# Retention attention and a gated feed-forward layer in one kernel: another layout for the fourth block, another order in the queues

## The chip, the cores and the metric

The kernel runs on one core of a Trainium2 chip. The metric is the time of one execution on the device in microseconds (us); a comparison takes the median of several runs. A profile of one execution gives the times of the single instructions. TensorE (PE) multiplies matrices, VectorE (DVE), ScalarE (ACT) and GpSimd (POOL) work on elements, SyncE (SP) issues most of the DMA transfers.

## The reference

q, k and v have 8 batches, 8 heads, 576 positions and 64 columns in float32. Scores are q times k transposed over the root of 64, each multiplied by gamma(head) to the power of the distance and cut to the causal half; they multiply v. The result, as 4608 tokens of 512 columns, goes through a layer of 2048 hidden columns with h * cos(h):

```python
ret = scores * Dmat[None, :, :, :]          # gamma ** (i - j) for i >= j, else 0
x = np.matmul(ret, v).transpose(0, 2, 1, 3).reshape(4608, 512)
h = x @ w_in
out = (h * np.cos(h)) @ w_out
```

## The kernel before

The 4608 tokens are cut into 18 blocks j of 256 tokens (two chunks of 128), and into nine tiles n of 512 tokens (blocks 2n and 2n + 1) for the feed-forward layer. Blocks are counted from 0 here, so the fourth block is block 3.

For each block: load (L135 and L149) brings q, k and v in float32 through SyncE's queue; prep (scaled, L167) multiplies q and k by powers of gamma on GpSimd into bf16 tile qks; round_v (L178) makes v bf16; a transpose makes qkT from qks, either as one DMA of SyncE (transpose_dma, L197) or as eight TensorE transposes for each of q and k with a copy out of PSUM (transpose_pe, L210 and L215). scores (L244 or L282) multiplies keys with queries into PSUM, and VectorE multiplies by the mask into ret (L255 and L262, or L292). sums_of (L319) multiplies keys with values; VectorE adds the result to a running sum (L338, or L349 for each chunk), which ScalarE rounds into sb (L359). out_own (L375) multiplies ret with v, out_carried (L407) multiplies queries with the rounded sum, both into one PSUM bank, which outputs copies into xT on ScalarE (L430).

Blocks below NP_B hold two neighbouring tokens of k and v in a partition ("pair"): one DMA with pieces of 512 bytes, and 64 rows in each matmul of sums and own parts. The others hold one key and value a partition: a DMA for each chunk with pieces of 256 bytes, and 128 rows in a matmul. q always has two tokens a partition.

For each tile n: mm1 (L445) multiplies x with w_in, ScalarE makes cos (L457), VectorE multiplies both into gT (L460). The second product (mm2_seven, product, L563) works on a two by two split of gT and w_out with seven products in the order given by xs; w_sums and g_sum (L503) make the sums of quarters that it needs. g_sum runs on VectorE, but one of the four sums of each tile runs on GpSimd in pieces of two: number 3 for n = 1 and number 7 for n above 1. The tile n = 0 takes a plain second product instead (L927), with todo naming what else is issued after how many of its matmuls, and ends in copies of four row groups to tiles ot (L937).

Results leave through tiles ot of a pool of two buffers for each tag:

```python
op = ctx.enter_context(tc.tile_pool(name="op", bufs=2))
```

For n = 0 the four row groups take tags "a", "b", "c", "d" in turn. For n = 1, where products run in the order 2, 4, 6, 5, 7, 3 after an earlier 1, copied (L593, ScalarE) takes c11 from tag "a", p2 from "d", c21 from "c", u1 from "b" and c22 from "d"; adds (L589) follow on VectorE, and store issues two DMAs of SyncE for each (L579).

The schedule is written by hand: every engine runs its instructions in the order in which the program issues them, and waits only on semaphores. step(j) issues prep, the DMA transpose and round_v of the next block and then the load of a later one; sums_after(n, i) issues pieces of sums after the i-th group of mm1; at[...] puts scores, sums and outputs of the next blocks ahead of single products. A DMA on SyncE uses one of eight semaphores in turn, and waits for the DMA eight before it.

Of the kernel before, what the change touches and what calls it, by code (L numbers as in the profile page):

```python
# [13 lines left out]
ALU = mybir.AluOpType  # L14
# [3 lines left out]
def kernel(  # L18
# [9 lines left out]
    nc = tc.nc  # L28
    P = 128
# [17 lines left out]
    last = NT - 1  # L47
    BK = 256
    NB = NTOK // BK
    NP_B = 4  # L50
    PERQ = 9
    PERK = 9
    MIX = PERK // 2
# [133 lines left out]
    def prep(j):  # L187
        for name in "kq" if j < NP_B else "qk":
            for y in range(2):
                scaled(nc.gpsimd, j, name, y)  # L190
# [12 lines left out]
    def transpose_pe(j, name, bank, evac, ys=(0, 1)):  # L203
        if ("qkT", j) not in tiles:
            new_qkT(j)
        m = "qk".index(name)
        ps = psum.tile([P, len(ys), HG, P], BF16, tag=bank, name="tr")
        for u, y in enumerate(ys):
            for hg in range(HG):
                nc.tensor.transpose(  # L210
                    ps[:, u, hg, :],
                    tiles["qks", j][:, m, y, hg].rearrange("s a d -> s (a d)"),
                    ident,
                )
        evac(tiles["qkT", j][:, m, ys[0] : ys[-1] + 1], ps)  # L215
# [13 lines left out]
    def scores(j, banks):  # L229
        cs = chunks[j]  # L230
        kT = tiles["qkT", j]
        ret = retp.tile([P, 2, HG, 2, P], BF16, tag="ret", name="ret")
        pss = [
            psum.tile([P, HG, 2, P], F32, tag=t, name="sc")
            if isinstance(t, str)
            else [psum.tile([P, HG, P], F32, tag=u, name="sc") for u in t]
            for t in banks
        ]
        if cs[0].pair:
            order = [(c, y, he, hg) for hg in range(HG) for y in range(2) for he in range(2) for c in cs]  # L240
            mask = mask_mix if any(c.mixed for c in cs) else mask_p
            for c, y, he, hg in order:
                ps = pss[he]
                nc.tensor.matmul(  # L244
                    ps[y][c.rows, hg, :] if isinstance(ps, list) else ps[c.rows, hg, y, :],
                    lhsT=kT[he * D : he * D + D, 1, y, hg, c.rows],
                    rhs=q_cols(c, he, hg),
                    start=True,
                    stop=True,
                )  # L250

            def masked(he):
                if isinstance(pss[he], list):
                    for y in range(2):
                        nc.vector.tensor_tensor(  # L255
                            out=ret[:, he, :, y, :],
                            in0=pss[he][y],
                            in1=mask[:, y].unsqueeze(1).to_broadcast([P, HG, P]),
                            op=ALU.mult,
                        )  # L260
                    return
                nc.vector.tensor_tensor(  # L262
                    out=ret[:, he].rearrange("p b r i -> p b (r i)"),
                    in0=pss[he].rearrange("p b r i -> p b (r i)"),
                    in1=mask.rearrange("p r i -> p (r i)").unsqueeze(1).to_broadcast(
                        [P, HG, 2 * P]
                    ),
                    op=ALU.mult,
                )
        else:  # L270
            ret = ret.rearrange("p a b r i -> p (a b r i)").rearrange(
                "p (k a b i) -> p k a b i", k=2, a=2, b=HG
            )
            pss = [
                ps.rearrange("p b r i -> p (b r i)").rearrange("p (a b i) -> p a b i", a=2, b=HG)
                for ps in pss
            ]
            for c in cs:
                for hg in range(HG):
                    for i0 in range(0, P, HP):  # L280
                        for he in range(2):
                            nc.tensor.matmul(  # L282
                                pss[c.k][i0 : i0 + HP, he, hg, :],
                                lhsT=kT[he * D : he * D + D, 1, c.k, hg, i0 : i0 + HP],
                                rhs=q_cols(c, he, hg),
                                start=True,
                                stop=True,
                            )

            def masked(k):  # L290
                mask = mask_cmix if cs[k].mixed else mask_c
                nc.vector.tensor_tensor(  # L292
                    out=ret[:, k].rearrange("p a b i -> p (a b) i"),
                    in0=pss[k].rearrange("p a b i -> p (a b) i"),
                    in1=mask.unsqueeze(1).to_broadcast([P, H, P]),
                    op=ALU.mult,
                )

        tiles["ret", j] = ret
        return [lambda: masked(0), lambda: masked(1)]  # L300
# [213 lines left out]
    def sums_after(n, i):  # L514
        if n == 1:
            slots = {5: ((5, 0, 4),), 6: ((6, 0, 4),)}
        else:
            slots = {
                2: ((7, 0, 4),),
                3: ((5, 0, 4),),  # L520
                4: ((6, 0, 4), (7, 4, 6)),
                5: ((3, 0, 4),),
                6: ((5, 4, 6), (7, 6, E2)),
            }
        for x in slots.get(i, ()):
            g_sum(n, *x)
# [46 lines left out]
    def stored_rows(r0, c0, c1, t, queues=(nc.sync, nc.sync)):  # L573

        rows = out[r0 : r0 + P * t.shape[1], c0:c1].rearrange(
            "(j i r) c -> r i j c", r=2, i=HP
        )
        for r in range(2):
            queues[r].dma_start(rows[r], t[r * HP : (r + 1) * HP])  # L579
# [85 lines left out]
    def load_next(**kw):  # L665
        nonlocal loaded
        if loaded < NB:
            load(loaded, **kw)
            loaded += 1

    def step(then_load=True):

        nonlocal prepared
        if prepared < NB:
            prep(prepared)
            transpose_dma(prepared)
            round_v(prepared)
            prepared += 1
            if then_load:
                load_next()  # L680

    def steps_to(j):
        while prepared < min(NB, j):
            step()
# [128 lines left out]
    w_dma.append(load_w_out(12))  # L813
    scaled(nc.gpsimd, 2, "q", 0)
    load_next(names="kqv", gate=w_dma[6])
    load_next()
    prepared = 4

    def intro(j, sc_banks, st_bank, put_off=None, then=None):
        add = sums_of(j, st_bank)  # L820
# [44 lines left out]
    for n in range(NT):  # L865
        blocks = blocks_of.get(n) or [(e + k * E2, 0, W) for e in range(0, E2, 2) for k in range(2)]
        for i, (et, c0, cw) in enumerate(blocks):
            inside = {
                (0, 1): {2: block1_carried},
                (1, 0): {2: lambda: transpose_pe(3, "q", "b", act)},  # L870
                (1, 2): {3: block3_scores},
                (1, 3): {2: lambda: sums_of(3, "st")()()},
            }.get((n, i), {})
            off = [] if (n, i) == (1, 3) else None
            between = block1_sums if (n, i) == (0, 0) else None
            mm1(n, et, c0, cw, banks_of.get(n, "abmabmab")[i], inside, off, between)
            if (n, i) == (0, 0):
                block1_own()
            if (n, i) == (1, 0):
                step(False)  # L880
                load_next()
                for r0, ot in stores:
                    stored_rows(r0, 0, DM, ot)
            if (n, i) == (1, 1):
                step(False)
                load_next()
                step()
            if (n, i) == (1, 3):
                mm2_seven(1, {}, None, (1,), lambda: (outputs(3, "m"), off.pop()()))
            if n:  # L890
                sums_after(n, i)
            if (n, i) == (2, 6):
                step()
        if n == 0:
            gT = tiles["g", n]
            two = psum.tile([P, 2, DM], F32, tag="m", name="o")
# [6 lines left out]
                (37, lambda: round_v(2)),  # L903
                (42, block2_scores),
                (50, block2_sums),
                (50, lambda: prep(3)),
                (57, load_next),
                (59, lambda: round_v(3, (act, act))),
                (60, lambda: outputs(2, "b")),
                (62, lambda: transpose_pe(3, "k", "a", act)),  # L910
            ]
            todo += [
                (at, lambda x=x, e=e: w_sums(x, e, e + 4))
# [51 lines left out]
        def first_scores(flush, pend):  # L965
            g_sum(n, 5, 4, E2)
            g_sum(n, 6, 4, E2)
            masks = scores(a, "ab")
            add_a = sums_of(a, "st")
            add_b = sums_of(b, "m")  # L970
            masks[0]()
            add_a()()
            masks[1]()
            g_sum(n, 3, 0, E2)
            g_sum(n, 7, 0, 4)
            tiles["rounded"] = add_b()
            g_sum(n, 7, 4, E2)

        def next_scores(flush, pend):
            outputs(a, "a")  # L980
# [30 lines left out]

        def stored(u):
            if n == 1:
                steps_to({2: 8}.get(u, 0))
            else:
                steps_to({0: 2 * n + 6, 3: 2 * n + 7}.get(u, 0))

# [31 lines left out]
```

## Time and profile before

| | |
|---|---|
| median of three runs | 296.8 us (295.59 to 297.94) |
| profiled execution | 296.28 us, span 294.6 us |
| granted TensorE clock, mean | 0.994 |
| busy: PE, DVE, ACT, POOL | 283.2, 215.6, 143.0, 145.6 us |
| DMA queue of SyncE | 44.84 MB, 75.6% of 16 engines over the span |
| DMA transposes | 14, median 5.1 us from issue to landing |

The span is the time from the first to the last instruction of the profile; the rest of the execution's time lies around it. Busy times count work only, not waiting or the issue of DMAs. A timeline row gives start, duration, engine, line, operation, output<-inputs, shape and count, and in brackets the idle time of the engine before it with what ended it. Lines are those of the kernel before.

### The profile page before, as it was taken

The page shows a single profiled execution, that of the slowest core. Times are in us where ns is not written, and L with a number is a line of the kernel's source. Part 1 is how long each engine was busy: PE and PEld are TensorE (multiplying, and loading weights), DVE is VectorE, ACT ScalarE, POOL GpSimd, SP SyncE. Part 2 cuts the span into 40 slices and gives each one's busy share as a digit, 9 for nine tenths or more (in the row PEclk, how much of TensorE's full clock was granted, in tenths as well). Part 3 has the DMA queues.
Part 4 walks back from the last instruction along what each step waited for, and adds up shares of the span by engine and source line. Part 5 has one row for each costly group of instructions (what it writes and reads, how often), then busy time and mean ns, then how long its engine had stood idle before and what let it go on. Part 6 is the DMA issues. An engine that isn't in the chain of part 4 may idle for free.

```text
span 294.6 us, 7623 instructions
## 1 busy us (share of the span) xinstructions
PE 283.2 (96%) x3248; PEld 195.0 (66%) x3268; DVE 215.6 (73%) x268; ACT 143.0 (49%) x166; POOL 145.6 (49%) x172
## 2 busy tenths in 40 slices
PE   7889999999999999999999999999999999999993
PEld 2568755878864688458845884588458845874583
DVE  4585748558986999699659965996599659835933
ACT  4466537646436624563356335633563356326620
POOL 8641535847864495839713961497148014102400
PEclk9799999999999999999999999999999999999999
DMA  7999999999899999999999999979930630121014
GB/s 197 268 222 215 232 247 214 231 181 231 198 199 227 204 240 210 191 219 197 236 203 193 243 215 197 219 128 223 203 64 21 127 71 0 38 65 44 2 37 107
DMA packets 128930, 49.78 MB, mean 169 GB/s; under 512 B 89344, under 2 KB 128384, under 8 KB 128896
## 3 DMA queue, kind: packets, MB, share of 16 engines
q1 hardware_dynamic: 124288, 44.84, 75.6%
q0 software_dynamic: 4224, 4.19, 8.8%
q8 instruction: 25, 0.41, 0.6%
q10 hardware_dynamic: 384, 0.26, 0.4%
q14 instruction: 9, 0.07, 0.1%
HBM read 36.70 MB, written 9.44 MB: 157 GB/s over the span
## 4 chain that ended last, share of the span: by engine, by line
PE 79%; DVE 10%; DMA 4%; POOL 2%; ACT 2%; issue 1%; DVEq 0%; ACTq 0%
PE h L445 38%; PE o L563 27%; PE o L927 5%; DVE gT L460 3%; PE ov L375 3%; DVE gs L503 3%; DMA qkT<-qks 2%; PE st L319 2%; POOL qks L167 2%; PE sc L282 2%; DVE ret L292 2%; PE ov L407 1%; DMA fk<-in_k_dram 1%; PE tr L210 1%; ACT cosh L457 1%
## 5 line engine op out<-in xcount | busy, mean ns | idle before, releaser
L445 PE MATMUL h<-xT,w_in_sb 128*128 128x512 bf16 (+1 forms) x690 | 126.6, 340 | 1.0
L460 DVE TENSOR_TENSOR gT<-h,cosh 128x1024 bf16<-128x1024 f32 x72 | 87.9, 1221 | 37.5 <-ACT cosh L457 37.4
L457 ACT ACTIVATE cosh<-h,half_pi 128x1024 f32<-128x1024 f32 x72 | 80.2, 1114 | 66.4 <-PE h L445 65.1
L445 PEld LDWEIGHTS <-w_in_sb 128*128 128x128 bf16 x704 | 68.4, 98 | 55.3 <-issue 0.6
L503 POOL TENSOR_TENSOR gs<-gT 128x512 bf16<-128x512 bf16 x28 | 35.8, 1280 | 92.2 <-DVE gT L460 92.2
L563 PEld LDWEIGHTS <-gs 128*128 128x128 bf16 x528 | 49.5, 98 | 6.4
L167 POOL TENSOR_TENSOR qks<-fq,gq 128x512 bf16<-128x512 f32 x31 | 33.9, 1113 | 18.1 <-DMA fq<-in_q_dram 14.9
L563 PEld LDWEIGHTS <-gT 128*128 128x128 bf16 x384 | 37.1, 98 | 6.3
L593 ACT COPY ot<-o 128x512 f32<-128x512 f32 x33 | 19.3, 586 | 40.5 <-PE o L563 40.5
L167 POOL TENSOR_TENSOR qks<-fk,gkc 128x512 bf16<-128x512 f32 x28 | 31.8, 1154 | 0.0
L589 DVE TENSOR_TENSOR ot<-ot,o 128x512 f32<-128x512 f32 x35 | 23.2, 680 | 10.9 <-ACT ot L593 7.9
L563 PE MATMUL o<-w_out_sb,gs 128*128 128x256 bf16 (+1 forms) x264 | 30.6, 269 | 0.0
L563 PE MATMUL o<-ws,gs 128*128 128x256 bf16 (+1 forms) x264 | 30.5, 270 | 0.0
L563 PE MATMUL o<-w_out_sb,gT 128*128 128x256 bf16 x256 | 30.5, 273 | 0.0
L292 DVE TENSOR_TENSOR ret<-sc,mask_c 128x1024 bf16<-128x1024 f32 x25 | 29.7, 1214 | 0.1
L430 ACT CAST xT<-ov 128x1024 bf16<-128x1024 f32 x16 | 16.2, 1013 | 11.0 <-PE ov L407 11.0
L178 POOL CAST vb<-fv 128x512 bf16<-128x512 f32 x31 | 18.7, 624 | 5.7 <-DMA fv<-in_v_dram 5.6
L503 DVE TENSOR_TENSOR gs<-gs,gT 128x1024 bf16<-128x1024 bf16 x16 | 15.7, 982 | 0.3
L503 DVE TENSOR_TENSOR gs<-gT 128x512 bf16<-128x512 bf16 (+1 forms) x25 | 15.4, 615 | 0.4
L563 PE MATMUL o<-ws,gT 128*128 128x256 bf16 x128 | 15.3, 273 | 0.0
L349 DVE TENSOR_TENSOR s<-st,s 128x256 f32<-128x256 f32 x18 | 7.6, 421 | 10.4 <-PE st L319 10.1
L359 ACT CAST sb<-s 128x512 bf16<-128x512 f32 (+1 forms) x18 | 10.3, 573 | 9.3 <-DVE s L347 3.8
(81 smaller groups left out, 203.4 us busy)
## 6 DMA issues: line engine op xcount, KB each, us to landing
out_dram<-ot SPq DMA_DIRECT2D x69, 128.0 KB, 2.6
fk<-in_k_dram SPq DMA_DIRECT2D x25, 256.0 KB, 5.7
fv<-in_v_dram SPq DMA_DIRECT2D x25, 256.0 KB, 5.1
fq<-in_q_dram SPq DMA_DIRECT2D x12, 512.0 KB, 5.3
w_in_sb<-in_moe_w_in_dram POOLq DMA_DIRECT2D x4, 512.0 KB, 8.1
w_out_sb<-in_moe_w_out_dram POOLq DMA_DIRECT2D x4, 512.0 KB, 9.8
fk<-in_k_dram SPq DMA_DIRECT2D x3, 512.0 KB, 5.3
fv<-in_v_dram SPq DMA_DIRECT2D x3, 512.0 KB, 7.0
```

The lines of the kernel that those rows point to most:

```text
L167: return eng.tensor_tensor(out=dst.rearrange("p b a d -> p a b d"), in0=src.rearrange("p (a b) d -> p a b d", a=2), in1=by.rearrange("p (a ...
L178: runs[y](vb[:, y], f[:, :, y, :] if j < NP_B else f[:, y])
L292: nc.vector.tensor_tensor(out=ret[:, k].rearrange("p a b i -> p (a b) i"), in0=pss[k].rearrange("p a b i -> p (a b) i"), in1=mask.unsqueez ...
L430: evac(x, ps)
L445: nc.tensor.matmul(ps[:, j, :], lhsT=w_in_sb[:, dg, (et + j) * P : (et + j + 1) * P], rhs=xT[:, dg, c0 : c0 + w], start=(dg == 0), stop=(d ...
L457: nc.scalar.activation(cosh, ps, ACTF.Sin, bias=half_pi, scale=1.0)
L460: nc.vector.tensor_mul(gT[:, et : et + m, c0 : c0 + w], ps, cosh)
L503: i = eng.tensor_tensor(out=tiles["gs", n, x][:, e : e + step], in0=a[:, e : e + step], in1=b[:, e : e + step], op=op_,)
L563: nc.tensor.matmul(dst[i], lhsT=lhs[:, e, j * P : (j + 1) * P], rhs=rhs[:, e, c0:c1], start=(fresh and e == 0 and (i == 0 or len(parts) > 2)),
L589: return lambda: nc.vector.tensor_tensor(out=out_, in0=in0, in1=in1, op=ALU.add)
L593: nc.scalar.copy(t, tiles["all", x])
L927: nc.tensor.matmul(pss[t], lhsT=gT[:, e, t * P : (t + 1) * P], rhs=w_out_sb[:, e, :], start=(e == 0), stop=(e == ET - 1),)
```

## The change

Four things change.

1. NP_B goes from 4 to 3, so block 3 holds one key and value a partition. Its k and v are loaded by two DMAs each, its prep goes by q first, and scores of such blocks may now use two half banks for a chunk (masked then works on each half). The gate on a load of w_out, which load puts on the first DMA of a pair block or of q, stands on q's DMA instead of k's for this block.
2. Block 3's qkT is made by a DMA transpose instead of two groups of TensorE transposes. For this, load 4 is split: q and k before it, v after it in SyncE's order.
3. The eight stores of n = 0 are issued after the steps of blocks 5 and 6 (the transposes of the sixth and seventh blocks and loads 7 and 8), no longer ahead of them.
4. GpSimd's sums: for n = 1 number 3 is issued after number 7, and its first piece waits for VectorE's last piece of number 7; for n = 2 number 7 is issued in one run after the seventh group of mm1, and the step of block 8 is issued before it, in n = 1.

```diff
-    NP_B = 4
+    NP_B = 3
...
             for c in cs:
...
-                                pss[c.k][i0 : i0 + HP, he, hg, :],
+                                pss[c.k][he][i0 : i0 + HP, hg, :],
...
+                if isinstance(banks[k], str):
+                    runs = [(ret[:, k].rearrange("p a b i -> p (a b) i"), whole[k], H)]
+                else:
+                    runs = [(ret[:, k, he], pss[k][he], HG) for he in range(2)]
+                for to, ps, n in runs:
+                    nc.vector.tensor_tensor(
+                        out=to,
+                        in0=ps,
+                        in1=mask.unsqueeze(1).to_broadcast([P, n, P]),
+                        op=ALU.mult,
+                    )
...
             slots = {5: ((5, 0, 4),), 6: ((6, 0, 4),)}
+        elif n == 2:
+            slots = {3: ((5, 0, 4),), 4: ((6, 0, 4),), 5: ((3, 0, 4),), 6: ((5, 4, 6), (7, 0, E2))}
...
     load_next(names="kqv", gate=w_dma[6])
-    load_next()
-    prepared = 4
+    load(4, "qk")
+    loaded, prepared = 5, 4
...
-                (1, 0): {2: lambda: transpose_pe(3, "q", "b", act)},
...
             if (n, i) == (1, 0):
                 step(False)
                 load_next()
-                for r0, ot in stores:
-                    stored_rows(r0, 0, DM, ot)
             if (n, i) == (1, 1):
                 step(False)
                 load_next()
                 step()
+                for r0, ot in stores:
+                    stored_rows(r0, 0, DM, ot)
...
-            if (n, i) == (2, 6):
-                step()
...
-                (50, lambda: prep(3)),
+                (50, lambda: (prep(3), transpose_dma(3), load(4, "v"))),
...
-                (62, lambda: transpose_pe(3, "k", "a", act)),
...
             masks[1]()
-            g_sum(n, 3, 0, E2)
             g_sum(n, 7, 0, 4)
             tiles["rounded"] = add_b()
-            g_sum(n, 7, 4, E2)
+            i = g_sum(n, 7, 4, E2)
+            g_sum(n, 3, 0, E2, gate=i)
...
-                steps_to({2: 8}.get(u, 0))
+                steps_to({2: 8, 3: 9}.get(u, 0))
```

More of the change, by code (lines that the diff above doesn't have):

```diff
@@ L273, in scores @@
             )
+            whole = [
+                None if isinstance(ps, list) else ps.rearrange("p b r i -> p (b r) i") for ps in pss
+            ]
             pss = [
-                ps.rearrange("p b r i -> p (b r i)").rearrange("p (a b i) -> p a b i", a=2, b=HG)
+                ps
+                if isinstance(ps, list)
+                else [
+                    ps[:, he * HG // 2 : (he + 1) * HG // 2].rearrange("p b r i -> p (b r) i")
+                    for he in range(2)
+                ]
                 for ps in pss
@@ L291, in masked @@
                 mask = mask_cmix if cs[k].mixed else mask_c
[L292 to L297, printed above, removed]
+                if isinstance(banks[k], str):
[9 more added lines that the diff above has]
+                    )
         tiles["ret", j] = ret
```

## The prediction

> **What bounds the kernel now.** I read the page first, then TensorE's waits, the chain that ended last, and last the timelines of the engines around the change. The page:
>
> ```profile
> span 294.6 us, 7623 instructions
> PE 283.2 (96%) x3248; PEld 195.0 (66%) x3268; DVE 215.6 (73%) x268; ACT 143.0 (49%) x166; POOL 145.6 (49%) x172
> PE 79%; DVE 10%; DMA 4%; POOL 2%; ACT 2%; issue 1%; DVEq 0%; ACTq 0%
> ```
>
> TensorE works 96% of the span; apart from the first 17 us and the last 5 us its waits are 0.4 us or less each. So only two things move the time: matmuls taken out of TensorE's stream, or a wait long enough to empty it. The change does both, and the second is in the queue of stores. These are SyncE's DMA issues in the stage of n = 1:
>
> ```profile
> 65.87 2.99 SPq L149 DMA_DIRECT2D fv<-in_v_dram  x3
> 68.96 5.81 SPq L579 DMA_DIRECT2D out_dram<-ot  x8
> 74.88 2.27 SPq L197 DMA_TRANSPOSE qkT<-qks  x1
> 77.19 0.84 SPq L135 DMA_DIRECT2D fq<-in_q_dram  x1
> ...
> 84.42 3.26 SPq L197 DMA_TRANSPOSE qkT<-qks  x1
> 87.73 0.58 SPq L135 DMA_DIRECT2D fq<-in_q_dram  x1
> ...
> 90.71 3.04 SPq L149 DMA_DIRECT2D fv<-in_v_dram  x2
> 93.85 3.14 SPq L579 DMA_DIRECT2D out_dram<-ot  x4
> ```
>
> The eight stores of n = 0 stand after the load of block 6 and ahead of the transpose of block 5 (74.88), load 7, the transpose of block 6 (84.42) and load 8. Landings come from the view of DMA issues, narrowed to one issue each; its last column is us from issue to landing:
>
> ```profile
> fv<-in_v_dram SPq DMA_DIRECT2D x1, 128.0 KB, 4.7
> out_dram<-ot SPq DMA_DIRECT2D x1, 128.0 KB, 2.6
> fv<-in_v_dram SPq DMA_DIRECT2D x1, 256.0 KB, 4.6
> ```
>
> These are the last piece of load 6 (issued 68.22, landed 72.9), the last of the eight stores (74.17, 76.8) and the last piece of load 8 (92.52, 97.15). ScalarE, which reuses that store's buffer:
>
> ```profile
> 79.96 0.59 ACT L593 COPY ot<-o 128x512 f32<-128x512 f32 x1 [1.16 <-PE o L563]
> 80.78 1.01 ACT L430 CAST xT<-ov 128x1024 bf16<-128x1024 f32 x1 [0.23 <-PE ov L407]
> 81.69 0.62 ACT L359 CAST sb<-s 128x512 bf16<-128x512 f32 x1
> 85.00 1.01 ACT L430 CAST xT<-ov 128x1024 bf16<-128x1024 f32 x1 [2.70 <-PE ov L407]
> ```
>
> The copy at 79.96 is c22 of n = 1 (copied("d", 5)). Tag "d" has two buffers: the last rows of n = 0 took the first, p2 the second, so c22 writes the first again and must wait until its store has landed. That was 76.8, so 3.2 us of slack hide this wait today. Behind the copy, in ScalarE's order, stand x of block 4, the rounded sums sb for block 5, and x of block 5. On TensorE:
>
> ```profile
> 83.53 0.41 PE L375 MATMUL ov<-ret,vb 128*64 128x128 bf16 x8
> 84.19 0.41 PE L375 MATMUL ov<-ret,vb 128*64 128x128 bf16 x8 [0.25 <-DVE ret L292]
> 84.53 0.42 PE L407 MATMUL ov<-qkT,sb 64*64 64x128 bf16 x16
> 84.88 1.92 PE L563 MATMUL o<-w_out_sb,gs 128*128 128x256 bf16 x16
> 86.64 13.98 PE L445 MATMUL h<-xT,w_in_sb 128*128 128x512 bf16 x62
> ```
>
> Block 5's own part (L375) writes bank "a", which x of block 4 empties; its carried part (L407) reads sb; the first products of n = 2 (86.64; in the chain their long run starts at 86.80) read both x.
>
> **The change, part by part.** *Taken from TensorE:* block 3's two groups of transposes (L210, 50.95 and 52.70, 0.45 each: 0.90); its sums become 16 matmuls instead of 32 (0.74 in the chain at 46.35 for a block with 32, 0.37 at 133.24 for one with 16: 0.37); its own part likewise (0.87 from 62.15 to 63.03 against 0.45: 0.42). Scores stay 32 matmuls. Together 1.69 us. About 1.1 come back at once: the first x of n = 1 (ScalarE 50.53 to 51.55) is no longer covered by transposes (0.2), and block 3's carried part follows sb, which hangs on VectorE's run from 57.01 to 62.3 (0.9).
>
> *The transpose of block 3 on the DMA* must land before its scores (57.01, now about 56.2). The gate on w_out's load moves from k to q (the split load of k has none), so k comes early and q lands near 43.5 (5.3 us after 38.15) instead of 45.25. GpSimd's four multiplies (2.04 a pair) end near 47.6, as now; the transpose, behind load 4's q and k, lands near 54. No wait, with 2 us to spare.
>
> *GpSimd's sums.* Those of n = 1 (74.50, 5.44) now follow VectorE's last sum. VectorE's sums beside them shorten from 1.5 to 0.7 twice, which can remove waits of 0.38 and 0.25 on TensorE; the last piece would end near 85 and cost product 3 0 to 0.4. Those of n = 2 follow the ninth block's multiplies and end near 103, needed at 108.49: nothing. All of this, net about -1 us, lies ahead of the stall below and is swallowed by it.
>
> *The stores moved past two transposes and two loads.* They come behind load 8. When does load 8 land? Today 97.15. Off: the eight stores (72.9 to 76.8) 3.85; the gap after them, since load 7's q landed 4.3 after its transpose where load 8's q needed 1.7: 2.5; the earlier block 3: 1.8; load 5 in 6.0 instead of 6.8, as load 8: 0.8. On: the new transpose 3.5 (block 6's landed 3.5 after the load ahead; others added 2.6 to 3.85); 256-byte pieces for block 3's k and v 0.3; a gap of 1.9 after that transpose, because SyncE waits for the multiplies before it may issue load 4's v. That makes 93.9. The eight stores then end 3.85 later, as behind load 6: the awaited one lands at T = 97.8. Bounds: 94.5 (a transpose at 2.6, no new gap, a little more kept) to 102 (neither the earlier block 3 nor the gap after the stores is won).
>
> The Trainium skill (DMA: Bandwidth & Descriptors, section Latency and other measured facts) puts a DMA transpose at 261 GB/s. By it block 3's 0.52 MB would take 2.0 us, T would be 96.3 and the time 311.8; every transpose in this trace added 2.6 us or more, and the sum goes by the trace.
>
> *From T on:* the copy starts x of block 4 0.5 us later, sb 0.9 after that for 0.62, the carried part 0.35, product 3 1.85, with some 0.1 of handing over: n = 2 starts at T + 4.3 at full clock. TensorE stands idle from about 82.5 until x of block 4 is out at T + 1.6, 17 us, and I expect half clock then:
>
> ```profile
> 5.06:8.47 3.41, 1.97 (x18) 1.00 1.16 290
> 8.47:11.89 3.42, 3.42 (x71) 0.50 1.18 279
> 11.89:15.30 3.41, 2.55 (x51) 1.00 1.20 259
> ```
>
> (Columns: window, us, PE busy, clock granted, DMA share, GB/s.) A window 58% busy was followed by one at half clock, a full one by full clock. So the restart runs at half for 2.0 to 5.4 us and loses half of that: 1.9 (1.0 to 2.7).
>
> n = 2 starts at 97.8 + 4.3 + 1.9 = 104.0 instead of 86.8: +17.2. Afterwards nothing is late: the ninth block's transpose lands at 115.14 now, held TensorE 0.2 us (won back), and in the changed kernel lands near 118 and is wanted near 132. From 115 to the end TensorE has no gaps, so the delay stays whole. Sum: +17.0 on the profiled execution's 296.28 (span 294.6, 1.7 around it) gives 313.3; that execution lies 0.5 under the median, and I say 313.5.
>
> **Rivals.** *No wait (7%):* if the buffer of c22 is free in time, the kernel is not slower. It decides at the copy: the store would have to land by about 79.5. For it: no wait shows there today. Against: the two buffers of tag "d" and the 18 us of queue ahead of the stores. Time: -1.69 (matmuls) + 1.1 (given back) - 0.6 (VectorE's waits) + 0.2 (GpSimd's last sum) = -1.0, so 295.3, as long as the ninth transpose lands before 114; it could be up to 3 us late.
> *Short stall (6%):* SyncE, not the transfers, sets the pace. The shortest issue rows (transpose 2.2, q 0.6, k 1.2, v 2.0) from 47.6 on add up to 29; with the stores' 5.8 and 2.0 to landing T = 84.5, n = 2 starts near 90.5: 300. Against: issues now take 2 to 3.5 us because the queue is full, and the 16 DMA engines are busy in nearly all of the first 180 us.
> *Long stall (7%):* the twelve stores in a row hold SyncE (0.6 us each), transfers contend more, T passes 102 and the clock stays low for two windows: 319 to 322.
>
> **How the numbers follow.** The forecast has 80%. T from 94.5 to 102 gives 310 to 317.5, the clock's bounds widen that to 309 and 318.3; taking in a little of the neighbours, 307.5 to 318.5. A measurement here tells about 1% (3 us) from no change: only the first rival stays within that or falls below. Slower 0.92, same 0.06, faster 0.02.
>
> **What would show it.** Right: ScalarE's copy of c22 starts near 98 with over 15 us idle before it, released by the store's DMA; TensorE idle from about 82 to 99, then 0.50 granted for one window; the long run of n = 2 from about 104; the time from there to the end as before. The transpose of block 3 lands before its scores, and the sums of n = 2 on GpSimd hold nobody. Wrong: the copy starts near 80, or TensorE waits at block 3's or block 8's scores instead.

## The result, and the profile after

| | before | after |
|---|---|---|
| median | 296.64 us (295.59 to 297.94) | 317.5 us (317.25 to 317.88) |
| profiled execution | 296.28 us, span 294.6 | 317.37 us, span 315.7 |
| granted TensorE clock, mean | 0.994 | 0.968 |

The changed kernel takes 1.0702 times the time of the kernel before (95% interval 1.0657 to 1.0746), 20.9 us more. The forecast was 313.5 us, from 307.5 to 318.5.

The page of the changed kernel:

```profile
span 315.7 us, 7550 instructions
PE 285.3 (90%) x3220; PEld 194.3 (62%) x3220; DVE 217.3 (69%) x269; ACT 141.1 (45%) x164; POOL 146.4 (46%) x172
PE 77%; DVE 7%; DMA 6%; SPq 4%; POOL 2%; ACT 2%; issue 1%; DVEq 0%; ACTq 0%; POOLq 0%
```

TensorE is busy longer (285.3 against 283.2 us) with 28 matmuls fewer, and its share fell from 96% to 90%. The new idle time is almost one single wait, in TensorE's view of waits (total, times, longest, in us; three of its lines):

```profile
PE ov L388 <- ACT xT L443: 19.5, 1, 19.5
...
PE sc L290 <- DMA qkT<-qks: 1.0, 1, 1.0
PE ov L420 <- ACT sb L372: 0.7, 1, 0.7
```

ScalarE's timeline shows who is late. The first row is the copy of c22, the second x of block 4, the third the sums sb for block 5, the last x of block 5:

```profile
101.20 0.59 ACT L608 COPY ot<-o 128x512 f32<-128x512 f32 x1 [22.68 <-DMA out_dram<-ot]
101.68 1.02 ACT L443 CAST xT<-ov 128x1024 bf16<-128x1024 f32 x1
102.59 0.63 ACT L372 CAST sb<-s 128x512 bf16<-128x512 f32 x1
104.44 1.01 ACT L443 CAST xT<-ov 128x1024 bf16<-128x1024 f32 x1 [1.22 <-PE ov L420]
```

Before, this copy ran at 79.96 after a pause of 1.16 us for its product. Now ScalarE does nothing for 22.68 us, and what ends the pause is the store of the buffer. TensorE's timeline:

```profile
81.30 1.92 PE L578 MATMUL o<-w_out_sb,gs 128*128 128x256 bf16 x16
102.75 1.06 PE L388 MATMUL ov<-ret,vb 128*64 128x128 bf16 x16 [19.53 <-ACT xT L443]
103.74 0.64 PE L420 MATMUL ov<-qkT,sb 64*64 64x128 bf16 x16
104.31 3.60 PE L578 MATMUL o<-w_out_sb,gs 128*128 128x256 bf16 x16
107.70 4.54 PE L458 MATMUL h<-xT,w_in_sb 128*128 128x512 bf16 x19
```

The long run of n = 2 starts at 107.70 instead of 86.64. From there to the end of the span it is 208.0 us, and it was 208.0 before (294.6 less 86.64). So the whole loss, 21.1 us, has happened by the start of n = 2. The same 16 matmuls of a product take 1.92 us ahead of the stall and 3.60 behind it.

SyncE's issues in this stage:

```profile
74.77 3.65 SPq L197 DMA_TRANSPOSE qkT<-qks  x1
...
84.72 3.50 SPq L197 DMA_TRANSPOSE qkT<-qks  x1
...
91.02 2.60 SPq L149 DMA_DIRECT2D fv<-in_v_dram  x2
93.66 10.11 SPq L594 DMA_DIRECT2D out_dram<-ot  x12
103.89 2.21 SPq L197 DMA_TRANSPOSE qkT<-qks  x1
```

The eight stores, which went out from 68.96 before, now follow load 8, in one row with the next four. The view of DMA issues, narrowed to one issue each, for the last piece of load 8 (issued 92.54), the eighth store (98.71) and block 3's q (38.51):

```profile
fv<-in_v_dram SPq DMA_DIRECT2D x1, 256.0 KB, 4.9
...
out_dram<-ot SPq DMA_DIRECT2D x1, 128.0 KB, 2.4
...
fq<-in_q_dram SPq DMA_DIRECT2D x1, 512.0 KB, 7.8
```

They landed at 97.47, 101.10 and 46.26. The copy starts 0.10 after the eighth store has landed. Last, the clock, in windows laid on its own steps (window, us, PE busy and count, PEld, DVE, ACT, POOL, granted clock, DMA share, GB/s):

```profile
84.40:87.77 3.37, 0.00 (x0) 0.00 (x0) 0.00 (x0) 0.00 (x0) 3.37 (x4) 1.00 1.46 191
87.77:91.20 3.43, 0.00 (x0) 0.00 (x0) 0.00 (x0) 0.00 (x0) 3.43 (x5) 0.50 0.86 204
...
101.40:104.80 3.40, 2.05 (x35) 1.59 (x35) 1.29 (x2) 2.18 (x4) 0.00 (x0) 0.50 0.42 100
104.80:108.25 3.45, 3.45 (x17) 2.32 (x16) 0.30 (x1) 0.65 (x1) 0.00 (x0) 0.50 0.96 186
108.25:111.70 3.45, 3.45 (x18) 1.56 (x17) 0.98 (x2) 1.18 (x2) 0.00 (x0) 1.00 1.16 256
```

One window without matmuls is followed by half clock. A window 60% busy (2.05 of 3.40) doesn't bring the full clock back, a full one does.

### The profile page after: what moved, and what is told of

Read it like the earlier page. It is cut to its first block, busy times and chain, and to the rows that moved or that the text cites. A ratio compares the mean times of both kernels' runs of the same rounds, so it can differ in the third digit from the quotient of the medians.

```text
span 315.7 us, 7550 instructions
## 1 busy us (share of the span) xinstructions
PE 285.3 (90%) x3220; PEld 194.3 (62%) x3220; DVE 217.3 (69%) x269; ACT 141.1 (45%) x164; POOL 146.4 (46%) x172
## 4 chain that ended last, share of the span: by engine, by line
PE 77%; DVE 7%; DMA 6%; SPq 4%; POOL 2%; ACT 2%; issue 1%; DVEq 0%; ACTq 0%; POOLq 0%
PE h L458 36%; PE o L578 29%; DMA fq<-in_q_dram 4%; PE o L938 3%; PE ov L388 3%; PE sc L290 2%; DVE gs L516 2%; PE ov L420 2%; DMA qkT<-qks 2%; PE st L332 2%; DVE ret L305 2%; DVE gT L473 1%; SPq L594 1%; SPq L149 1%; POOL gs L516 1%; DVE ret L262 1%
## 5 line engine op out<-in xcount | busy, mean ns | idle before, releaser
L578 PEld LDWEIGHTS <-gs 128*128 128x128 bf16 x528 | 50.2, 99 | 7.4 <-DVE gs L516 0.2
L167 POOL TENSOR_TENSOR qks<-fq,gq 128x512 bf16<-128x512 f32 x31 | 34.7, 1139 | 14.6 <-DMA fq<-in_q_dram 8.4
L167 POOL TENSOR_TENSOR qks<-fk,gkc 128x512 bf16<-128x512 f32 x30 | 34.6, 1173 | 0.0
L305 DVE TENSOR_TENSOR ret<-sc,mask_c 128x1024 bf16<-128x1024 f32 (+1 forms) x28 | 32.1, 1177 | 0.6 <-PE sc L290 0.5
L578 PE MATMUL o<-w_out_sb,gs 128*128 128x256 bf16 (+1 forms) x264 | 32.3, 278 | 0.0
L388 PE MATMUL ov<-ret,vb 128*64 128x128 bf16 (+1 forms) x336 | 12.4, 225 | 20.2 <-ACT xT L443 19.5
L388 PEld LDWEIGHTS <-vb 128*64 128x64 bf16 (+1 forms) x336 | 9.3, 112 | 22.1 <-issue 21.5
L362 DVE TENSOR_TENSOR s<-st,s 128x256 f32<-128x256 f32 x20 | 8.4, 421 | 10.4 <-PE st L332 10.1
```

Source lines behind the costliest of these rows:

```text
L167: return eng.tensor_tensor(out=dst.rearrange("p b a d -> p a b d"), in0=src.rearrange("p (a b) d -> p a b d", a=2), in1=by.rearrange("p (a ...
L305: nc.vector.tensor_tensor(out=to, in0=ps, in1=mask.unsqueeze(1).to_broadcast([P, n, P]), op=ALU.mult,)
L388: nc.tensor.matmul(ps[h % 2 * D : h % 2 * D + D, h // 2, c.c0 : c.c0 + P], lhsT=vb[c.rows, y, h, :], rhs=rhs, start=part not in begun, sto ...
L578: nc.tensor.matmul(dst[i], lhsT=lhs[:, e, j * P : (j + 1) * P], rhs=rhs[:, e, c0:c1], start=(fresh and e == 0 and (i == 0 or len(parts) > 2)),
```

## Experiments

The theory: the stores moved past two transposes and two loads hold c22's buffer, and through ScalarE's order they empty TensorE. The rivals: the transpose of block 3 and its loads make the queue late whatever the stores do, GpSimd's sums cost by themselves, and the half clock has another cause than the idle time. Ratios are to the kernel before, with 95% intervals; it was run again beside each experiment, with medians from 296.56 to 296.81 us. Runs of one version differ among themselves too: with the changed kernel's order in the queue, load 8 landed at 97.47 in the changed kernel's profile and at 97.76 to 98.77 in four others (own buffer, reversed stores, 84 and 92 idle matmuls), so a landing that differs by less than 1.3 us shows nothing by itself.

**The stores back in their place, the rest of the change kept.**

```diff
                 step(False)
                 load_next()
+                for r0, ot in stores:
+                    stored_rows(r0, 0, DM, ot)
             if (n, i) == (1, 1):
...
-                for r0, ot in stores:
-                    stored_rows(r0, 0, DM, ot)
```

> The changed kernel with its third part undone: the eight stores of n = 0 stand ahead of the steps of blocks 5 and 6 again. Theory A (ScalarE's copy of c22 waits for the last of these stores, and all that is behind it on ScalarE waits too): the long stall is gone. The stores end 3.6 us after load 6, which lands at 78.8 in the changed kernel, so the copy waits until about 82.5 instead of 101.1. The transpose of block 5 then comes behind the stores, lands near 85.3 and holds the scores of block 5 (80.5) for some 4.8 us: about 301 us. Rival B (the DMA queue as a whole is late because of the new transpose and the split loads, and the copy's wait only goes along with it): the time stays above 310.

Measured: 303.5 us, 1.022 (1.0178 to 1.0262). So 14 us of the change hang on the place of the stores. What is left, about 7 us, hangs mostly on another wait, on TensorE, and the half clock behind it:

```profile
85.15 1.07 PE L290 MATMUL sc<-qkT 64*64 64x128 bf16 x32 [4.65 <-DMA qkT<-qks]
86.15 3.60 PE L578 MATMUL o<-w_out_sb,gs 128*128 128x256 bf16 x16
```

The queue is later than before by the new transpose and what comes with it. With the eight stores ahead of it, the transpose of block 5 landed at 85.11 (before 79.41), and block 5's scores wait 4.65 us for it. The clock then is half from 83.7 to 90.5. ScalarE's copy waits for its store here too, to 82.64, as the theory had it (82.5), but x of block 4 and sb are out before the scores can start.

**Only the stores moved, in the kernel before.** The edit is part 3 of the diff alone.

> The kernel before with the third part alone: the eight stores of n = 0 behind the steps of blocks 5 and 6, everything else as before. Theory A: in the trace of before load 6 lands at 72.9; one transpose, load 7, another transpose, load 8 and the stores after it put the awaited store at about 95.8, ScalarE's copy there, and the tile n = 2 at about 102 instead of 86.8: about 311.5 us, some 5 less than the changed kernel because the queue has no transpose of block 3. Rival B: without the new transpose and the split loads the queue is not late, 296 to 298 us.

Measured: 311.82 us, 1.0509 (1.0458 to 1.0561). ScalarE's copy:

```profile
97.34 0.59 ACT L593 COPY ot<-o 128x512 f32<-128x512 f32 x1 [18.88 <-DMA out_dram<-ot]
```

The same stall without any other part of the change, and close to the 311.5 us expected. Load 8 landed at 93.3, the eighth store at 97.24, n = 2 started at 103.84. Part 3 alone is worth 15 us; the kernel with everything else was 7 above.

**The eight stores in reverse order, in the changed kernel.** The awaited buffer's two stores then are the first, not the last.

```diff
-                for r0, ot in stores:
+                for r0, ot in stores[::-1]:
```

> The changed kernel with the eight stores of n = 0 in reverse order of row groups, so that the store of the buffer that c22 takes goes first of the eight and not last; the same bytes at the same place in the queue. Theory A: this store lands at about 98.1 instead of 101.1, the copy starts 3.0 us earlier and the time falls by as much: 314.5 us. Rival B: the queue is as long as before, nothing changes: 317.5 us.

Measured: 315.48 us, 1.0638 (1.0582 to 1.0693). The copy follows the second store instead of the eighth:

```profile
98.75 0.58 ACT L608 COPY ot<-o 128x512 f32<-128x512 f32 x1 [19.61 <-DMA out_dram<-ot]
```

That store landed at 98.65. The copy is 2.45 us earlier and the kernel 2.0 faster, a little less than expected (3.0), as load 8 landed 0.5 later here, at 98.00. The last of the eight stores now lands at 101.68, and nobody waits for it: the buffer named by the theory sets the time, not the row of stores.

**A buffer of its own for c22, in the changed kernel.** To make room, the zeros that idle matmuls read have 128 columns and are read four times, and the ones lie in scratch memory.

```diff
-            t = op.tile([P, 2, N2], F32, tag=tag, name="ot")
+            t = op.tile([P, 2, N2], F32, tag=tag, name="ot", **({"bufs": 1} if tag == "e" else {}))
...
-                c22 = copied("d", 5)
+                c22 = copied("e", 5)
```

> The changed kernel with a buffer of its own for c22 of n = 1, so that ScalarE's copy waits for no store; all queues keep the order of the changed kernel. (To make room, the zeros of the warming matmuls are 128 columns read four times, and the ones lie in a scratch buffer.) Theory A: the copy runs near 79.7 and the stall of 19.5 us is gone although the stores still land near 98 to 101. What is left: the scores of block 3 wait about 1 us for their transpose, product 3 a few tenths for GpSimd's sum, and the ninth block's transpose lands near 117.6 where the scores want it at 115: about 298.5 us. Rival B: the queue is as late as in the changed kernel, so the time stays above 310.

Measured: 305.15 us, 1.0291 (1.025 to 1.0332). ScalarE's copy waits only for its product, although the stores landed as late as 99.5 to 103.1:

```profile
78.96 0.59 ACT L615 COPY ot<-o 128x512 f32<-128x512 f32 x1 [1.16 <-PE o L585]
```

and n = 2 starts at 85.82, 0.8 earlier than in the kernel before. The stall of c22 is gone. Still 8.3 us are lost, 6.7 more than expected, most of it at the next thing that the late queue holds:

```profile
122.66 1.07 PE L297 MATMUL sc<-qkT 64*64 64x128 bf16 x32 [6.21 <-DMA qkT<-qks]
```

The ninth block's transpose landed at 122.6, not at the expected 117.6, and the clock is half behind this wait, from 120.03 to 126.86. Another 2.0 us are TensorE's waits for gT at the products of n = 2, which the run of part 4 alone below takes up. In the changed kernel this transpose landed at 120.1, and nobody waited, because the 21 us of stall lay ahead of it.

**Only parts 1 and 2, in the kernel before.** Block 3's layout, its transpose on the DMA and the split load 4; stores and sums as before.

> The kernel before with the first and second parts alone: block 3 with one key and value a partition, its transpose on the DMA, load 4 split; stores and sums as before. Theory A: the DMA queue carries one transpose more, load 6 lands near 78.5 instead of 72.9, the stores at 82.5, and the transpose of block 5 behind them at 85.1; TensorE waits some 4.6 us at the scores of block 5 and then runs at half clock for about 3 us. ScalarE's copy waits too, but not longer. About 302 us. Rival (the prediction's sum of matmuls taken out, 1.7, less what comes back): 295.5 us.

Measured: 301.71 us, 1.0174 (1.0133 to 1.0214). TensorE's waits:

```profile
PE sc L290 <- DMA qkT<-qks: 5.8, 2, 4.7
...
PE h L458 <- ACT xT L443: 1.4, 1, 1.4
```

The longest of them is block 5's scores again, at 86.38. So the matmuls that parts 1 and 2 save cost a late queue, and with the stores in their old place the two parts are a loss by themselves. Which of them makes the queue late, the layout with its pieces of 256 bytes or the transpose on the DMA, no run here separates.

**Only part 4, in the kernel before.**

> The kernel before with the fourth part alone: GpSimd's sums later in n = 1 and n = 2, and the ninth block's step in n = 1. The prediction held that this costs nothing (and wins 0.6 at most): 296 us. The run with a buffer of its own for c22 suggests another theory: GpSimd makes the four pieces of n = 2 in one run of 5 us, VectorE's sums beside it take 1.4 to 1.6 us instead of 0.7, gT comes late and TensorE waits some 2 us at the first products of n = 2. By that, less the 0.6 won in n = 1: 297.5 to 298.5 us.

Measured: 297.89 us, 1.004 (1.0005 to 1.0075). n = 2 starts at 85.27, 1.4 us earlier than before, as VectorE's sums of n = 1 have GpSimd no longer beside them: two of 128x1024 took 1.53 and 1.60 us before, and the same two take 0.98 and 0.67. Then this is lost again at the products of n = 2:

```profile
101.51 1.92 PE L565 MATMUL o<-w_out_sb,gT 128*128 128x256 bf16 x16 [0.95 <-DVE gT L460]
103.91 0.61 PE L565 MATMUL o<-w_out_sb,gT 128*128 128x256 bf16 x4 [0.48 <-DVE gT L460]
```

They wait for VectorE, which runs beside GpSimd's run of four sums; first GpSimd's row, then VectorE's:

```profile
98.62 5.12 POOL L503 TENSOR_TENSOR gs<-gT 128x512 bf16<-128x512 bf16 x4
```

```profile
101.37 1.34 DVE L503 TENSOR_TENSOR gs<-gT 128x512 bf16<-128x512 bf16 x1
...
104.35 0.69 DVE L503 TENSOR_TENSOR gs<-gs,gT 128x1024 bf16<-128x1024 bf16 x1
```

VectorE's sum of 128x512 took 0.42 us in the kernel before at this place (101.36), and takes 1.34 beside GpSimd's. The median is 1.1 us above that of the kernel before, with single times from 296.04 to 300.14: part 4 alone wins nothing, and may lose a little.

**The gate of w_out's load back on block 3's first k, in the changed kernel.**

```diff
+                        if gate is not None:
+                            after(i, gate)
+                            gate = None
```

> The changed kernel with the gate on w_out's load back on block 3's first k, as it stands for pair blocks, so that k is no longer issued 7 us earlier. The prediction held that the early k wins 1.8 us of the queue; by that, q of block 3 would now land near 48 and the awaited store 1.8 later: 319.3 us. The trace of the changed kernel suggests that k and w_out only share the DMA engines in that time (w_out's last piece landed at 43.6 instead of 41.6 and q at 46.3 instead of 45.3): by that q lands at 45.5 to 46.5 and the time stays at 317.5 or falls by up to 1 us.

Measured: 318.61 us, 1.0738 (1.0704 to 1.0772), 1.1 above the changed kernel. Neither view was right. k goes out at 38.55 instead of 31.20, and q still lands at 46.03 (46.26 in the changed kernel), load 4's k at 54.71 (54.90). Only behind that is the queue later: the transpose of block 3 landed at 58.64 (56.85), load 8 at 98.36 (97.47). So the early k wins nothing for q. Whether it wins the 0.9 us for load 8 and the stores isn't shown: with the early k too, load 8 landed as late as 98.77 in another run.

**84, then 92 idle matmuls in the stall, in the changed kernel.** They multiply zeros, and stand in TensorE's order between the last product ahead of the stall and block 5's own part, which waits for x of block 4.

```diff
         def last_outputs(flush, pend):
+            warm(92, "b")
             outputs(b, "a")
```

> The changed kernel with 84 idle matmuls of zeros (18 us) ahead of block 5's own part, where TensorE stands idle; nothing that the stall depends on is touched. Theory: the clock stays at full, block 5's own and carried parts and product 3 take 2.7 us instead of 4.95, so the time falls by about 2.2 us to 315.3 and no window shows half clock. Rival: the low rows after the stall come from something else than the idle time, and the time stays at 317.5.

> The changed kernel with 92 idle matmuls of zeros (19.6 us) ahead of block 5's own part; with 84 a gap of 2.4 us was left, and half clock still came for one window. From the start of ScalarE's copy of c22 to the first product of n = 2 the changed kernel takes 6.5 us (101.2 to 107.7). If the idle time alone lowers the clock, it stays full now and this takes 4.3 to 4.6 us, whatever the landing of the store: 315.5 us if that is at 101 again. If the clock falls for another reason, it takes 5.5 or more.

Measured: 318.4 us with 84 (1.0714, 1.0659 to 1.0769), 315.39 us with 92 (1.063, 1.0595 to 1.0664). The 84 were too few: the store landed at 102.44 in that execution, they left a gap of 2.43 us ahead of L388, and the clock was half for one more window. Its time decides nothing, as the store alone came 1.3 us later than in the changed kernel. But it shows that 2.43 us without matmuls can be enough: laid on the clock's own steps, the window from 102.01 to 105.43 was busy for 1.34 us, and the next one had half clock. The 92 reach up to the end of the stall:

```profile
103.01 0.64 PE L388 MATMUL ov<-ret,vb 128*64 128x128 bf16 x16
103.58 0.42 PE L420 MATMUL ov<-qkT,sb 64*64 64x128 bf16 x16
103.93 1.92 PE L578 MATMUL o<-w_out_sb,gs 128*128 128x256 bf16 x16
105.69 6.64 PE L458 MATMUL h<-xT,w_in_sb 128*128 128x512 bf16 x30
```

```profile
104.80:108.25 3.45, 3.45 (x22) 1.96 (x21) 0.69 (x1) 0.90 (x2) 0.00 (x0) 1.00 1.17 166
```

The clock stays full, and n = 2 starts 4.2 us after the copy (101.46) instead of 6.5. So it was the idle time that had lowered the clock, and that cost 2.3 us in these two executions, 2.1 between the medians.

**A version mended at three places:** the changed kernel with c22's own buffer, the n = 2 sums in their old slots, and the ninth block's transpose ahead of load 9.

```diff
-                c22 = copied("d", 5)
+                c22 = copied("e", 5)
...
-        elif n == 2:
-            slots = {3: ((5, 0, 4),), 4: ((6, 0, 4),), 5: ((3, 0, 4),), 6: ((5, 4, 6), (7, 0, E2))}
...
+            if (n, i) == (2, 4):
+                step(False)
+                load_next()
+                load_next()
...
-                steps_to({2: 8, 3: 9}.get(u, 0))
+                if u == 2:
+                    step(False)
```

> The changed kernel with three things mended: a buffer of its own for c22 of n = 1, GpSimd's sums of n = 2 back in their slots between the groups of mm1 (the ninth block's step between them), and the ninth block's transpose ahead of load 9 in the queue. If the waits found so far are all there is, the copy waits for nothing, no sum is slowed, and the ninth transpose lands near 112 where the scores want it at 115: n = 2 starts near 85.8 instead of 86.8 and keeps that, 295.4 us, 1 us under the kernel before. If the DMA queue stays late elsewhere (blocks 9 to 11), 297 to 303.

Measured: 301.29 us, 1.0141 (1.0096 to 1.0186), so the second of the two expectations (297 to 303). The profiled execution, 303.77 us, was the slowest of the six, and only two things are read from it. The ninth transpose landed in time, at 116.06, and the longest wait is at a later block:

```profile
148.75 1.07 PE L297 MATMUL sc<-qkT 64*64 64x128 bf16 x32 [2.56 <-DMA qkT<-qks]
```

In this execution, then, the queue stays late, and with one wait taken away the next transpose is waited for. That the other five lose their 2.1 to 5.1 us at the same place is likely and not shown.

**The best of part 4 without the rest:** the kernel before, with GpSimd's n = 1 sums placed as in the change, and the ninth transpose ahead of load 9.

```diff
-            if (n, i) == (2, 6):
-                step()
+            if (n, i) == (2, 4):
+                step(False)
+                load_next()
+                load_next()
...
-            g_sum(n, 3, 0, E2)
...
-            g_sum(n, 7, 4, E2)
+            i = g_sum(n, 7, 4, E2)
+            g_sum(n, 3, 0, E2, gate=i)
...
-                steps_to({2: 8}.get(u, 0))
+                if u == 2:
+                    step(False)
```

> The kernel before with half of the fourth part, and the ninth transpose moved: in n = 1 GpSimd's sum follows VectorE's last one, the sums of n = 2 keep their slots, and the ninth block's step stands two groups earlier with its transpose ahead of load 9. With the whole fourth part n = 2 started at 85.3 instead of 86.6, and VectorE beside GpSimd's single run of sums lost 1.4 of it again. If that run was the reason, n = 2 keeps 0.7 to 1.4 us: 295.4 to 296.0 us. If the ninth block's multiplies beside VectorE cost as much, or a later transpose comes late, 296.5 to 298.

Measured: 296.36 us, 1.0007 (0.9977 to 1.0038): no difference that these runs can tell. No version here beats the kernel before.

## Why the prediction was right, and which terms were off

**The mechanism** held in each step from the store to the start of n = 2. The copy of c22 waits for the last of the eight stores, x of block 4, sb and x of block 5 stand behind it, TensorE is empty, and nothing of it is won back after the start of n = 2. The buffer of its own, the reversed stores and the stores alone show it by three different edits. The size came out 4.0 us too small, 1.0 below the upper end of the range: T was 3.3 late, the way from T to n = 2 took 0.4 more, and the rest lies in how the start of n = 2 was read before (86.80 against 86.64) and in the 0.2 that were to be won back.

**T, the landing of the awaited store,** was forecast at 97.8 (94.5 to 102) and came at 101.10. The mis-sized terms are in the ledger of load 8 (93.9 forecast, 97.47 measured); the 3.85 for the eight stores behind it came as 3.63. By its own terms the ledger has load 5 ending 3.1 later than before (3.5, 0.3 and 1.9 on, 1.8 and 0.8 off), at 64.3; it landed at 67.59. In this execution three terms make up the difference:

- "the earlier block 3: 1.8" failed. q landed at 46.26, not 43.5, since it took 7.8 us from its issue; w_out's load, which k now runs beside, landed at 43.63 instead of 41.64. From q to the end of load 4's k the same bytes took 8.64 us, 7.27 before. So load 4's k came 2.4 later (54.90 against 52.52) where the terms made it 1.5 earlier (1.8 off, 0.3 on): 3.9 us. The run with the gate on k shows 8.68 from q to that k with a late k, and the run with the own buffer 7.09 with an early one, so it isn't the early k that stretches it. Whether the 256-byte pieces do was not tested alone.
- The transpose and the gap after it were priced 3.5 and 1.9; together they and v added 2.85 (v ended 4.74 behind k, 1.89 before): 2.55 us better. Block 3's transpose landed 1.96 behind load 4's k. Here the figure of the Trainium skill (DMA: Bandwidth & Descriptors, section Latency and other measured facts), 261 GB/s for a transpose with a non-contiguous middle dimension, which gave 2.0, was nearer than the 3.5; in the runs with the own buffer and the reversed stores the same transpose came 2.96 and 3.88 behind, and the 3.5 was nearer. The sentence that every transpose in the trace of before added 2.6 us or more was a wrong reading: those issued at 133.87, 144.59, 158.71 and 169.38 landed 1.71 to 1.85 behind the transfer ahead.
- "load 5 in 6.0": it took 7.95, with one step of 2.3 us between two pieces (64.18 to 66.48). The run with only the stores moved has a step of 2.3 us there too (61.14 to 63.43), without block 3's transpose, and the kernel before has none. Its cause stays open.

3.9 less 2.55 plus 1.95 is 3.3. The first two terms share their parts differently in the four other runs with this order in the queue: load 4's k landed at 53.26 to 55.01 and the transpose 1.92 to 3.88 behind it, but v ended at 59.44 to 60.03 (59.64 here) where the terms give 58.3, and load 5 took 7.50 to 7.95. So two things are firm: block 3's loads and its transpose together came 1.1 to 1.7 us later than priced, and load 5 took 1.5 to 1.95 us longer.

From load 5 to load 8 the forecast was 29.6 us and 29.88 were measured. That is luck: the terms are off and cancel. The transposes of blocks 4, 5 and 6 landed 4.90 in all behind the loads ahead of them, where the sum kept the 9.94 of before; load 6 took 9.61 instead of 7.87 and load 8 7.26 instead of 6.00. "The gap after them: 2.5" was hardly won: load 7 took 8.10 where it had taken 8.28. So T stayed below 102, the bound for neither gain coming, because other terms fell out better than they were priced.

**From T on,** the forecast was 6.2 us, 4.3 at full clock and 1.9 for the half clock; it took 6.60. Without the half clock the 92 idle matmuls gave 4.2 us from the copy. The half clock cost 2.1 to 2.3 us, inside the bounds (1.0 to 2.7) but above the middle, because the restart ran 5.5 us at half (102.75 to 108.25), just beyond the 2.0 to 5.4 that were allowed for. One window of half clock after the stall was named as a sign; there were two, the first of them 60% busy.

**The smaller steps.** "No wait, with 2 us to spare" for block 3's scores was wrong: GpSimd's two pairs of multiplies started later, behind q, and took 2.49 and 2.94 instead of 2.04:

```profile
46.33 2.49 POOL L167 TENSOR_TENSOR qks<-fq,gq 128x512 bf16<-128x512 f32 x2 [5.05 <-DMA fq<-in_q_dram]
48.78 2.94 POOL L167 TENSOR_TENSOR qks<-fk,gkc 128x512 bf16<-128x512 f32 x2
```

The transpose was issued at 51.75 and landed at 56.85, forecast 54, and the scores waited 0.99. Block 3's wait for sb came as 0.66 (forecast 0.9), that for x as 0.2 (forecast 0.2). For GpSimd's n = 2 sums "nothing" held in the changed kernel only because the stall hid it: without the stall TensorE waited 2.0 us there (own buffer), and in the run of part 4 alone it undid the 1.4 won at n = 1, where the forecast had 0.6. That the ninth transpose harms nobody held, for the same reason.

**The rivals.** "No wait" fell, and its price would have been wrong too: with c22's buffer free the kernel takes 305, not 295.3, since its condition, the ninth transpose ahead of 114, isn't met (122.6). Up to the start of n = 2 its sum was close, 0.8 us earlier against 1.0. "Short stall" fell: T was 101, not 84.5. "Long stall" came nearest among the rivals, as T ended 0.9 us short of its 102 and the clock was low for two windows, as it said; but the twelve stores in a row (10.11 us of SyncE) held no one in the changed kernel who had not waited already.

## What to carry to other kernels

Before a store is moved back in an in-order queue, find the next writer of its buffer and what stands behind that writer on its engine; the slack is the store's landing to that write, here 3.2 us against the 18.6 us from load 6's landing to load 8's in the changed kernel (78.83 to 97.47). The queue of this kernel already delivered its transposes just in time; what was added to it was paid at the next transpose that somebody waited for, and mending one wait showed the next. A step that costs nothing inside a stalled kernel has to be priced again without the stall.

## What the runs showed of the hardware

- VectorE's bf16 sum of 128x512 took 0.42 us while GpSimd was idle (103.89 in the run of part 4 alone), and 1.34 beside a run of GpSimd's bf16 sums, three times as long. In the kernel before one took 1.02 beside GpSimd's multiplies (103.06), so the longer time isn't seen beside GpSimd's sums alone.
- Half clock followed a single empty window of 3.4 us, but also windows that were busy in part: 0.24 us of work (80.27 to 83.69 in the run with the stores back), 1.34 us (102.01 to 105.43 with 84 idle matmuls) and 1.97 us (5.06 to 8.47 in the kernel before). A window with 2.28 us of work (80.94 to 84.36, changed kernel) was not followed by it. One full window ended it; windows 60% busy (changed kernel) and 57% busy (1.95 of 3.40 from 83.7, in the run with the stores back) were followed by another half one. The Trainium skill (TensorE: Matmul & The Clock Gate, Part 1) says that the full clock comes after at least one busy short window and goes after an idle one, of some 3.4 us. The trace agrees for the full and the empty windows; that windows busy for 1.34 and 1.97 us lost the clock too goes beyond the rule.
- A k issued 7.3 us earlier on the same queue, while w_out's load was under way, brought the q behind it no sooner (46.26 against 46.03).
